# Converting three quarters of a feed-forward's weights inside the feed-forward itself, with the sums on two engines and another turn of the banks

## The chip, the cores and the metric

The kernel runs on one core of one Trainium2 chip. The metric is the device time of one execution in microseconds (us). TensorE is called PE, its weight loads PEld, VectorE is DVE, ScalarE is ACT, GpSimd is POOL, and SP is the queue that issues nearly all DMA.

## The reference

Attention with normalized queries and keys, then a feed-forward with a squared ReLU over the same tokens.

```python
batch, n_heads, seq, head_dim = (8, 12, 448, 64)
n_tokens, d_model, d_ff = (3584, 768, 2048)

q_n, k_n = rmsnorm(q, g_q), rmsnorm(k, g_k)
scores = scale * np.matmul(q_n, k_n.transpose(0, 1, 3, 2))
attn = softmax(scores)                       # written out, with 1e-9 in the denominator
x = np.matmul(attn, v)                       # (B,H,S,D) -> (B*S, H*D), in float32
h = np.maximum(x @ w_in, 0.0)
out = (h * h @ w_out).astype(np.float32)     # w_in and w_out are float64
```

The two weight matrices arrive as 64-bit floats. The kernel computes in 32-bit ones and converts the bits itself. Both matrix products of the feed-forward are done in seven block products in place of eight, which needs sums of weight blocks as well.

## The kernel before

The program has four units of two batches each. Attention of unit u runs interleaved with the feed-forward of unit u-1. Attention of unit 0 has no feed-forward beside it, and that is where all weights are converted. The four feed-forwards are called FFN 0, 1, 2 and the last one. Each has four blocks, and a block has *first products* (w_in, 14 products of 448 columns) and *second products* (w_out).

A piece is a block of 384 x 256 or 128 x 768 32-bit words (384 KB). There are 64 of them, four for each of 16 weight tiles. The conversion of a piece is a chain over four queues: a DMA loads the words, ScalarE and GpSimd split and clip them, VectorE joins them.

```python
    def split_words(n):
        ...
        low, high = words[n][:, :, :, 0], words[n][:, :, :, 1]
        nc.scalar.activation(high.bitcast(F32), high.bitcast(F32), AF.Copy, scale=REBIAS)
        nc.gpsimd.tensor_scalar(out=high.bitcast(F32), in0=high.bitcast(F32),     # the clip
                                scalar1=MOST, scalar2=-MOST, op0=ALU.min, op1=ALU.max)
        nc.scalar.activation(low.bitcast(F32), low, AF.Copy, scale=2.0**-29, bias=2.0**23)
        low_words[n] = ffn_p.tile([P, NK, P], U32, name="low", tag="part", bufs=4)
        nc.scalar.activation(low_words[n], low.bitcast(F32), AF.Copy, bias=-(2.0**23))

    def join_words(n):
        ...
            nc.vector.tensor_scalar(out=bits, in0=high, ...)                  # shift left, shift right
            nc.vector.scalar_tensor_tensor(out=bits, in0=high, ..., in1=bits) # sign
            nc.vector.tensor_tensor(out=bits, in0=bits, in1=low, op=ALU.add)
        ...
        if form == 3:                        # the fourth piece of a tile
            make_weight_forms(kind, targets.pop((kind, t)), t)   # four sums, then a store to DRAM

    def convert(n):                          # 64 times during attention of unit 0, the rest at once after it
        join_words(n - LAG)                  # LAG = 3
        load_weights(n + 2 * NT - LAG + 1)   # words: seven buffers, borrowed from acc
        split_words(n)
        make_sum()                           # one of the four sums, always on GpSimd
```

A finished tile goes to DRAM. Every feed-forward, FFN 0 too, loads its tiles from there two ahead. The products of a step turn through four PSUM banks:

```python
    def turn_roles():
        x, v_, w, y = roles
        roles[:] = w, y, v_, x               # at the start of every step
    PRODUCTS = {"P1": (0, True, ...), "P2": (2, True, ...), "P3": (1, False, ...), "P4": (3, True, ...),
                "P5": (1, True, ...), "P6": (0, False, ...), "P7": (0, False, ...)}   # role, first, ...
    FIRST_ORDER = ["P1", "P5", "P6", "P4", "P3", "P7", "P2"]
```

The feed-forward is a generator, and the main loop draws products from it between attention steps, by a cost of 2008 units for one feed-forward. This loop so also sets the order in which each engine is given its work. One place where that order shows in the trace of the kernel before: a ScalarE conversion (L574) waited 4.27 us for VectorE and ran at 94.16 us, and the exponentials issued after it ran at 94.62 us.

## Time and profile before

| | before |
|---|---|
| median of 3 runs, us | 1701.81 (1701.72 to 1702.39) |
| span of the profiled run, us | 1698.6 |
| mean granted clock of PE | 0.974 |
| attention of unit 0 with all conversions | up to 271.5 |
| FFN 0, FFN 1, FFN 2, from the last to the end, us | 386.7, 383.5, 382.1, 274.8 |

The lengths of the feed-forwards are differences between the starts of their first products in the trace. The page's totals for PE, PEld, VectorE, ScalarE and GpSimd (busy us, share of the span, instructions), and PE's waits over the whole run (what waits, for what: us in sum, times, longest), which bear on the bank turn:

```profile
PE 1567.1 (92%) x5204; PEld 710.7 (42%) x5204; DVE 794.4 (47%) x1138; ACT 552.1 (33%) x1033; POOL 643.9 (38%) x522
```

```profile
PE bank L451 <- POOL hid L423: 13.1, 7, 3.4
PE bank L402 <- DVE hid L421: 12.7, 16, 1.1
...
PE bank L451 <- DVE hid L421: 7.6, 9, 1.1
```

PE is busy 92% of the span, so there are about 130 us to win at most without fewer products or a higher clock, and most of them lie in the first 270 us. L402 is the first product, L451 the first of the second products, which needs the hidden layer (hid) complete. L402 itself does not read hid. In the program L421 reads the bank that L402 is to write next, so I take the 12.7 us to be a wait for that bank.

### The profile page before, as it was taken

What the parts mean: (1) busy time and instruction counts of PE and PEld (TensorE: products, weight loads), DVE (VectorE), ACT (ScalarE), POOL (GpSimd) and SP (SyncE); (2) the same over time, 40 slices, a digit from 0 to 9 for tenths busy, and PEclk for the clock granted to TensorE, in tenths of its full rate; (3) what the DMA queues carried; (4) which work ended last, traced back from release to release, by engine and by line L of the source; (5) the groups of instructions that cost most, each with busy time, mean ns of one, the idle gap of its engine ahead of it and who ended that gap; (6) DMA issues with size and microseconds to landing.
All of it is one profiled execution on the core that took longest, in us unless ns stands there. A gap on an engine that the chain in (4) does not pass through costs nothing.

```text
span 1698.6 us, 15053 instructions
## 1 busy us (share of the span) xinstructions
PE 1567.1 (92%) x5204; PEld 710.7 (42%) x5204; DVE 794.4 (47%) x1138; ACT 552.1 (33%) x1033; POOL 643.9 (38%) x522
## 2 busy tenths in 40 slices
PE   5877777999989999999999999999999999999997
PEld 2222222444434444444444444444444444545544
DVE  3878895334535355333535355433534344223323
ACT  5776662333231323333231323333231321220120
POOL 4666674524242245424243245434143232120211
PEclk9888888999999999999999999999999999999999
DMA  5687766222220315222221315222221314131112
GB/s 154 217 266 238 238 196 241 81 96 82 91 92 22 123 49 172 91 97 82 88 78 40 123 49 172 86 97 87 76 82 42 118 38 161 44 139 74 65 74 68
DMA packets 101081, 188.25 MB, mean 111 GB/s; under 512 B 49284, under 2 KB 83076, under 8 KB 90756
## 3 DMA queue, kind: packets, MB, share of 16 engines
q1 hardware_dynamic: 100992, 187.20, 32.6%
q8 instruction: 43, 0.70, 0.2%
q14 instruction: 42, 0.34, 0.1%
q10 hardware_dynamic: 4, 0.00, 0.0%
HBM read 152.57 MB, written 34.60 MB: 110 GB/s over the span
## 4 chain that ended last, share of the span: by engine, by line
PE 82%; DVE 6%; POOL 5%; issue 4%; DMA 2%; ACT 2%; SPq 0%; POOLq 0%; DVEq 0%; ACTq 0%
PE bank L402 28%; PE bank L468 26%; PE bank L212 9%; PE bank L272 8%; PE bank L451 5%; PE bank L191 2%; PE bank L283 2%; POOL rr L167 2%; DVE rden L294 1%; DVE hid L421 1%; PE bank L279 1%; POOL hid L423 1%; DVE out_sb L588 1%; ACT wT L214 1%; DMA in_sb<-in_forms 1%
## 5 line engine op out<-in xcount | busy, mean ns | idle before, releaser
L402 PE MATMUL bank<-xT,in_sb 128*128 128x448 f32 x1344 | 528.0, 545 | 24.8 <-DVE hid L421 12.7
L402 PEld LDWEIGHTS bank<-xT,in_sb 128*128 128x128 f32 x1344 | 249.0, 190 | 280.0 <-issue 247.9
L214 ACT ACTIVATE wT<-bank,rr 112x448 f32<-112x448 f32 x384 | 221.4, 627 | 429.7 <-PE bank L212 428.1
L423 POOL TENSOR_TENSOR hid<-hid 128x448 f32<-128x448 f32 x128 | 120.3, 950 | 472.6 <-ACT hid L422 472.6
L167 POOL TENSOR_TENSOR rr<-ms,minus_half 112x16 f32<-112x16 f32 x48 | 152.1, 3169 | 360.8 <-DVE ms L163 350.3
L468 PE MATMUL bank<-out_sb,hid 128*128 128x384 f32 x768 | 274.6, 487 | 0.0
L500 DVE TENSOR_TENSOR acc<-acc,bank 128x384 f32<-128x384 f32 x324 | 173.8, 551 | 205.7 <-PE bank L468 164.7
L212 PE MATMUL bank<-qT,kT 64*112 64x448 f32 x768 | 218.4, 621 | 52.7 <-DVE qT L193 43.0
L294 DVE RECIPROCAL rden<-bank 128x448 f32<-128x448 f32 x48 | 142.0, 2957 | 156.0 <-PE bank L283 128.9
L468 PE MATMUL bank<-out_sb,sums 128*128 128x384 f32 x576 | 212.4, 491 | 0.0
L272 PE MATMUL bank<-wT,vt 112*64 112x448 f32 x768 | 197.9, 596 | 2.2 <-DVE xT L304 2.1
L468 PEld LDWEIGHTS bank<-out_sb,hid 128*128 128x128 f32 x768 | 144.7, 190 | 103.1 <-issue 5.3
L409 ACT COPY part<-bank 128x448 f32<-128x448 f32 x128 | 68.1, 532 | 329.7 <-PE bank L402 329.7
L421 DVE TENSOR_TENSOR hid<-bank,part 128x448 f32<-128x448 f32 x128 | 76.4, 618 | 202.8 <-PE bank L402 202.0
L468 PEld LDWEIGHTS bank<-out_sb,sums 128*128 128x128 f32 x576 | 105.6, 190 | 81.9 <-issue 13.4
L422 ACT ACTIVATE hid<-hid 128x448 f32<-128x448 f32 x128 | 72.4, 577 | 198.1 <-DVE hid L421 198.1
L212 PEld LDWEIGHTS bank<-qT,kT 64*112 64x112 f32 x768 | 60.0, 182 | 171.4 <-issue 90.2
L230 DVE TENSOR_TENSOR sum<-sum,wT 112x448 f32<-112x448 f32 x72 | 65.1, 904 | 140.0 <-ACT wT L214 137.1
L451 PE MATMUL bank<-out_sb,hid 128*128 128x384 f32 x256 | 91.5, 510 | 23.1 <-POOL hid L423 13.1
L230 POOL TENSOR_TENSOR sum<-sum,wT 112x448 f32<-112x448 f32 x72 | 87.8, 1220 | 59.3 <-ACT wT L214 56.2
L272 PEld LDWEIGHTS bank<-wT,vt 112*64 112x64 f32 x768 | 39.6, 139 | 139.0 <-issue 128.6
L193 DVE TENSOR_SCALAR qT<-bank,g 128x448 f32<-128x448 f32 x48 | 32.7, 682 | 120.1 <-PE bank L191 120.1
(53 smaller groups left out, 1093.1 us busy)
## 6 DMA issues: line engine op xcount, KB each, us to landing
out_sb<-out_forms SPq DMA_DIRECT2D x32, 1536.0 KB, 9.3
in_sb<-in_forms SPq DMA_DIRECT2D x32, 1344.0 KB, 6.0
words<-in_moe_w_in_dram SPq DMA_DIRECT2D x32, 384.0 KB, 4.4
words<-in_moe_w_out_dram SPq DMA_DIRECT2D x32, 384.0 KB, 4.4
out_forms<-out_sb SPq DMA_DIRECT2D x8, 1536.0 KB, 6.5
qk<-in_q_dram SPq DMA_DIRECT2D x48, 224.0 KB, 2.8
qk<-in_k_dram SPq DMA_DIRECT2D x96, 112.0 KB, 3.0
vt<-in_v_dram SPq DMA_DIRECT2D x48, 224.0 KB, 2.7
```

Source lines behind the costliest of these rows:

```text
L167: nc.gpsimd.tensor_tensor(out=rr.rearrange("p x r -> p (x r)"), in0=ms, in1=minus_half.to_broadcast([CP, 4 * NJ]), op=ALU.pow,)
L212: nc.tensor.matmul(sc, lhsT=kT[r, ts(m, CP)], rhs=qT[r, :], start=True, stop=True)
L214: nc.scalar.activation(weights[i, e, m], sc, AF.Exp, scale=normal[i][2][:, 2 * m + e : 2 * m + e + 1])
L230: engine.tensor_tensor(out=sums[i, e], in0=sums[i, e], in1=weights[i, e, m], op=ALU.add)
L272: nc.tensor.matmul(av[ds(e * D, D), :], lhsT=values[i][:, e, m, :], rhs=weights[i, e, m], start=m == 0, stop=m == NJ - 1,)
L294: nc.vector.reciprocal(out=rden, in_=den)
L402: nc.tensor.matmul(ps, lhsT=w_sb[:, c, IN.index(left), :], rhs=forms[u, c][right], start=first and c == 0, stop=c == NK - 1, skip_group_ch ...
L421: nc.vector.tensor_tensor(out=dst, in0=ps, in1=part, op=op)
L423: nc.gpsimd.tensor_tensor(out=dst, in0=dst, in1=dst, op=ALU.mult)
L451: nc.tensor.matmul(ps, lhsT=flat[a][:, t, ds(FULL, P)], rhs=w_sb[t][:, 2 * a + half, :], start=a == 1 and t == 0, stop=a == 0 and t == 1,)
L468: nc.tensor.matmul(ps, lhsT=lefts[left][:, t, ts(tt, P)], rhs=w_sb[t][:, OUT.index(right), :], start=first and t == 0, stop=t == 1, skip_g ...
L500: nc.vector.tensor_tensor(out=acc, in0=acc, in1=ps, op=ALU.add)
```

## The change

The intent is to take conversions out of the stage in which every engine waits for another, and to do them where VectorE, ScalarE and GpSimd have room (busy for 44, 30 and 35% of FFN 0 before). Sixteen pieces (block 0's four tiles) stay in the first stage, one each 2.4 attention steps. The other 48 are drawn into FFN 0, one each 18 cost units (3.43 us on the average of FFN 0), straight into the tile that FFN 0 then uses. FFN 0 no longer loads its weights from DRAM, and finished tiles are still stored for the later ones.

```diff
     def load_in(n):
-        if n < B // 2 * NF // 2:
+        if NF // 2 <= n < B // 2 * NF // 2:         # load_out alike
...
-    def turn_roles():
+    def turn_roles(order):
         x, v_, w, y = roles
-        roles[:] = w, y, v_, x
+        roles[:] = (y, v_, w, x) if order is FIRST_ORDER else (w, y, v_, x)
...                                                  # and called at the end of a step
-        words[n] = ffn_p.tile([P, NK, P, 2], U32, name="words", tag="acc", bufs=2 * NT + 1)
+        words[n] = ffn_p.tile([P, HALF, 2], U32, name="words", tag="words")     # two buffers
...
-        low_words[n] = ffn_p.tile([P, NK, P], U32, name="low", tag="part", bufs=4)
-        nc.scalar.activation(low_words[n], low.bitcast(F32), AF.Copy, bias=-(2.0**23))
+        nc.scalar.activation(low, low.bitcast(F32), AF.Copy, bias=-(2.0**23))
...
+        (in_sb if kind == "in" else out_sb)[t] = dst       # the tile is used where it was made
...
-    def make_sum():
-        if sums_to_make:
+    def make_sums():
+        for engine in (nc.vector, nc.gpsimd) if sums_to_make else ():
             to, left, right, op = sums_to_make.popleft()
-            nc.gpsimd.tensor_tensor(out=to, in0=left, in1=right, op=op)
-            if len(sums_to_make[0]) == 2:
-                nc.sync.dma_start(*sums_to_make.popleft())
+            engine.tensor_tensor(out=to, in0=left, in1=right, op=op)
+        if sums_to_make and len(sums_to_make[0]) == 2:
+            nc.sync.dma_start(*sums_to_make.popleft())
...
+    def convert(more):
+        make_sums()
+        if begun:
+            join_words(begun.pop())
+        if more:
+            n = next(pieces)
+            load_weights(n + 1)
+            split_words(n)
+            begun.append(n)
...
+    early = deque(conversions(4, 0, 2.4))
+    block, product = COST // NBLK, 7 * COST_IN
+    late = deque(conversions(2, product + 2 * COST_IN, COST_IN))
+    for blk in range(1, NBLK):
+        late.extend(conversions(4 if blk < NBLK - 1 else 2, blk * block + 1, COST_IN))
...
                     spent += next(stream)
+                    while u == 1 and late and late[0][0] <= spent:
+                        convert(late.popleft()[1])
```

The layout of in_sb, the order of the four sums and the numbers of wT (12 to 10) and xT (33 to 32) buffers change as well. The words can't keep the buffers of acc, because FFN 0 uses those itself.

## The prediction

> **What bounds the kernel now.** I read the 40 slices of the span first, because they show where the regimes change.
>
> ```profile
> PE   5877777999989999999999999999999999999997
> DVE  3878895334535355333535355433534344223323
> ACT  5776662333231323333231323333231321220120
> PEclk9888888999999999999999999999999999999999
> ```
>
> A slice is 42.5 us. The first seven are another program than the rest: there PE is busy 70 to 80% at a clock of 0.8 to 0.9, with VectorE at 80 to 90%. From slice 8 on PE is at 90% or more and at full clock, and the other engines are half idle. So only the first 270 us, and what PE still waits for afterwards, can be shortened. Then I asked for busy time by stage: the stage of attention and weight conversion, the first feed-forward (FFN 0), and the second one.
>
> ```profile
> core 0: us, PE busy (x) PEld busy (x) DVE busy (x) ACT busy (x) POOL busy (x), PEclk, DMA share, GB/s
> 23.20:250.00 226.80, 174.26 (x652) 55.18 (x652) 183.68 (x258) 160.49 (x318) 149.81 (x147) 0.87 0.70 226
> 271.50:658.20 386.70, 376.43 (x1265) 171.79 (x1265) 169.38 (x239) 115.14 (x210) 135.99 (x101) 0.99 0.28 95
> ...
> 658.20:1041.70 383.50, 373.11 (x1264) 170.28 (x1264) 172.64 (x245) 115.13 (x210) 144.84 (x107) 1.00 0.27 91
> ```
>
> In the first stage VectorE is busy 184 of 227 us (81%), yet no engine is full: they wait on one another in turn. Who stops PE there is in the waits of PE up to 440 us:
>
> ```profile
> PE bank L212 <- DVE qT L193: 43.0, 12, 6.0
> PE bank L191 <- POOL qn L172: 13.9, 3, 9.1
> PE bank L402 <- DMA in_sb<-in_forms: 11.5, 1, 11.5
> ```
>
> Once for each pair of heads the scores wait 3.6 us for VectorE to copy qT out of its bank, because conversions stand ahead of that copy. FFN 0 then begins with a wait of 11.5 us for weights that come back from DRAM. What fills VectorE, ScalarE and GpSimd in that stage is in the groups by form, up to 265 us:
>
> ```profile
> L568 POOL TENSOR_SCALAR words<-words 128x384 f32<-128x384 f32 x64 | 37.6, 589 | 60.2 <-ACT words L567 60.2
> L574 ACT ACTIVATE low<-words 128x384 uint32<-128x384 f32 x64 | 35.8, 559 | 28.2 <-DVE in_sb L592 14.5 <-DVE out_sb L592 11.8
> L615 POOL TENSOR_TENSOR in_sb<-in_sb 128x384 f32<-128x384 f32 x32 | 35.5, 1109 | 11.4 <-DVE in_sb L592 11.4
> L588 DVE SCALAR_TENSOR_TENSOR out_sb<-words,out_sb 128x384 uint32<-128x384 uint32 x32 | 26.2, 819 | 1.1
> L592 DVE CUSTOM_DVE_ANT_0 out_sb<-out_sb,low 128x768 uint16<-128x768 uint16 x32 | 25.5, 797 | 2.0
> L584 DVE TENSOR_SCALAR out_sb<-words 128x384 uint32<-128x384 uint32 x32 | 17.0, 530 | 0.0
> ```
>
> All 64 pieces are converted there. With the rows of in_sb, a piece costs VectorE (17.2+17.0+21.9+26.2+21.1+25.5)/64 = 2.0 us, ScalarE 3 x 0.555 = 1.67 us, and GpSimd 0.59 us plus one sum of 1.1 us.
>
> [...]
> - [...] 0.87 is granted in the stage with the long waits, 1.00 in the dense one. [...]
> - [...] in the order of time L588 and L592 take 0.56 us alone and up to 1.24 us beside GpSimd[...].
> - [...] at 94.16 us a ScalarE conversion that had waited 4.27 us for VectorE ran before the exponentials of the next scores. This is the danger in the change.
> - [...] Over the whole run the first product of a feed-forward step waits 12.7 us in 16 waits for the hidden layer's evacuation.
>
> **The change, part by part.**
>
> (a) *First stage.* 16 of 64 pieces stay, one every 2.4 of 48 attention steps. VectorE's joins fall from 61 pieces to 16 in the window 23.2 to 250: 90 us less of its 184. What is left for a pair of heads (four steps): VectorE 2.96 (reciprocal) + 1.3 + 0.3 + 0.68 + 0.61 = 5.9 us, plus 1.67 pieces x 2.4 us = 9.9 us, so below PE. PE is then the bound. In the order of time around 42 to 53 us, at full clock, a plain step repeats every 2.6 us; the step with the turn of kT takes 3.8 us with its wait; the step with qT takes about 4.1 us. That is 13.1 us a pair. I add 0.7 us for joins that still stand before a qT copy (about half the pairs, 2 us each, in part hidden)[...]: 14.3 us. Before, 12 pairs take 226.8 us, 18.9 us each. Gain 12 x 4.6 = 55 us. The stretch from 250 to the first feed-forward product at 271.5 holds the 11.5 us wait for DRAM; the tiles are now used where they were made, so it goes: 11 to 12 us more. FFN 0 starts near 204 instead of 271.5: **-67 us** (50 to 85).
>
> (b) *FFN 0 takes 48 pieces.* They come one each 18 of 2008 cost units, and 383.5 us/2008 x 18 = 3.43 us. VectorE's own work in the first products of a block is about 0.35 (13.51 of 47.60 and 15.98 of 45.10 us, 18.8 of 45.6), or 1.2 us in that time. A piece adds 2.0 us and half a sum of some 0.75 us: 2.4 us. Together 3.6 us of work in 3.43 us. ScalarE has 1.0 + 1.67 = 2.7 us, GpSimd 1.2 + 0.6 + 0.55 = 2.4 us: they fit. So VectorE becomes the bound for these stretches, which are 1060 of the 2008 units. If it can run 90% full, a piece takes 4.0 us: 0.57 us x 48 = 27 us lost. **+28 us** (10 to 60).
>
> (c) *Words have two buffers.* A load may start only when the join before the last has ended, and its split on ScalarE comes one conversion later. The loop is split and clip 1.25 us, join 1.5 to 2.0 us, DMA 3.4 to 4.9 us to landing (read by windows), for two pieces: 3.1 to 4.1 us a piece. It is about as slow as VectorE, so I count it in the upper part of (b), not twice. The store of a finished tile (1344 KB, 5.8 us) stands ahead of each fourth load.
>
> (d) *Bank turn.* The first product of a step takes the bank of P4, copied long ago, instead of that of P2, evacuated last. This removes L402's 12.7 us and part of L451's 7.6 us on VectorE; L451's 13.1 us on GpSimd's square is a wait for data and stays. **-8 us**. It also gives VectorE the slack that (b) needs.
>
> (e) *Fewer weight buffers* (10 for 12): the new tile takes what the step before freed, and PE has run that before the new scores. 0 us. Loads of eight in and eight out tiles in FFN 0 go; they were hidden, apart from the first.
>
> Sum: 1701.8 - 67 + 28 - 8 = 1655.
>
> **Rivals.**
> 1. *FFN 0 gives it all back.* ScalarE stands at the head of its queue waiting for words, and the copies that free PE's banks stand behind. For: two buffers, a landing of up to 4.9 us, stores on the same queue[...]. Against: a copy of a product is needed only one or two products later, 2.2 to 4.5 us, so a ScalarE lag of 3 us is mostly absorbed. If the loop takes 4.9 us a piece, the loss is 70 us and the time about 1695.
> 2. *The conversions hide in FFN 0.* VectorE is at 44% over FFN 0 (169 of 387 us), and 48 x 2.4 = 115 us more makes 74%. With the new bank slack PE may never wait: 0 to 10 us lost, and 1630. Against: the average hides that the pieces come in stretches.
> 3. *The first stage stays slow*, bound by the chain of squares, GpSimd's power (3.1 us) and qn, or by qT behind the reciprocal (2.96 us) and a join. Then a pair takes 16 us, the gain is 47 us and the time 1675.
>
> **Range and chances.** The two large terms are unsure by some 17 and 25 us, nearly independent: about 30 us together. I take 1628 to 1690. The 2% line is at 1668, 13 us above my figure: faster 0.68, within 2% 0.29, slower 0.03.
>
> **What would show it.** (a) the first feed-forward product at 195 to 215 us, the clock before it above 0.92, L212's wait for qT under 25 us, no wait for in_sb from DRAM. (b) FFN 0 400 to 430 us long against 386.7, VectorE 65 to 75% over it, new PE waits of L402 on VectorE or ScalarE in it, and FFN 1 at 378 to 383 us. (c) ScalarE waiting for DMA of words by more than 40 us in sum would speak for rival 1. (d) L402's wait for hid under 4 us after FFN 0. The prediction is wrong if FFN 0 loses under 10 or over 60 us, or if a pair in the first stage takes over 16 us.

In (a) the 14.3 us a pair are 13.1 + 0.7 + 0.5 us; the 0.5 us, an allowance for a lower clock, was a guess. It is about 6 us over twelve pairs. The forecast itself stays: 1701.8 - 67 + 28 - 8 = 1655 us.

What the trace of the kernel before does show: PE was idle from 206.8 to 210.2 us, was granted a clock of 0.50 from there to 217.0 us, and of 1.00 from 217.0 to 223.8 us. Of its 64 instructions of L588, the 26 with no GpSimd instruction running at the same time took 0.56 us each; the other 38 took 0.88 us on average and 2.63 us at most. The 1.5 us for a join in (c) is one such undisturbed join of a w_out piece (L584, L588, L592: 0.35 + 0.56 + 0.56 us, from 93.99 us on).

## The result, and the profile after

| | before | after |
|---|---|---|
| median of 4 runs, us | 1701.76 (1699.97 to 1702.39) | 1708.47 (1706.47 to 1709.54) |
| span of the profiled run, us | 1698.6 | 1707.0 |
| first product of FFN 0 at | 271.5 | 208.6 |
| FFN 0 | 386.7 | 468.6 |
| FFN 1, FFN 2, last to end | 383.5, 382.1, 274.8 | 381.3, 377.6, 270.9 |

The ratio is 1.004, with a 95% interval of 1.0022 to 1.0057, so the times are the same within 2%. Here and below a ratio is the mean time of one kernel's fast runs over that of the other's fast runs of the same rounds, so not quite the ratio of the medians.

The sum closes: -62.9 (the earlier start) + 81.9 (FFN 0) - 2.2 - 4.5 - 3.9 = +8.4 us of span. Nothing failed in the first stage, and nothing was lost to the later feed-forwards. FFN 0 gave it all back.

The 40 slices of the changed kernel (42.7 us each, tenths of busy time, granted clock in the last line):

```profile
PE   5888897978969989999998999999998999999997
...
DVE  2654546476676556343534445343535444213323
ACT  4554443452441423333131223333132221220120
...
PEclk9999998988989989999999999999999999999999
```

VectorE's 8 and 9 tenths of the first slices are gone and the clock there is 0.9. In their place the sixth to the sixteenth slice, which are FFN 0, show PE at 6 to 9 with the clock dipping to 0.8, where before stood 9s with one 8. VectorE is at 7 at most in them.

The busy times of three stretches: the eleven pairs of heads of the first stage, FFN 0, and FFN 1.

```profile
core 0: us, PE busy (x) PEld busy (x) DVE busy (x) ACT busy (x) POOL busy (x), PEclk, DMA share, GB/s
23.10:186.80 163.70, 142.36 (x592) 46.96 (x592) 87.40 (x122) 89.74 (x166) 60.75 (x45) 0.93 0.37 109
208.60:677.20 468.60, 404.10 (x1266) 182.59 (x1264) 286.31 (x410) 182.89 (x354) 201.01 (x177) 0.92 0.33 108
677.20:1058.50 381.30, 374.99 (x1266) 171.97 (x1264) 172.70 (x245) 115.13 (x211) 144.56 (x106) 0.99 0.27 91
```

A pair of heads now takes 163.7/11 = 14.9 us, where the prediction had 14.3. FFN 0 and FFN 1 run the same 1266 matmuls, and FFN 0 takes 87 us more. Of these PE is idle for 64.5 - 6.3 = 58 us, and for 404.1 - 375.0 = 29 us it is busy longer with the same work, at a clock of 0.92 against 0.99. So each microsecond of added wait came with half a microsecond of slower work (29 to 58).

The blocks of FFN 0 one by one, from the second products of block 0 to the first products of block 3 (second and first in turn; the header is that of the lines above):

```profile
255.20:317.30 62.10, 50.43 (x169) 23.99 (x168) 36.74 (x47) 24.03 (x48) 22.84 (x18) 0.92 0.26 87
317.30:375.10 57.80, 50.09 (x139) 21.40 (x138) 36.56 (x57) 31.47 (x63) 30.20 (x30) 0.88 0.50 157
375.10:439.70 64.60, 53.07 (x169) 24.57 (x167) 42.17 (x60) 16.65 (x31) 23.33 (x20) 0.92 0.26 88
439.70:495.20 55.50, 48.78 (x143) 21.37 (x142) 38.90 (x55) 30.78 (x62) 24.14 (x26) 0.94 0.45 141
495.20:562.50 67.30, 53.32 (x165) 25.30 (x164) 43.25 (x64) 17.65 (x34) 29.92 (x23) 0.87 0.29 96
562.50:620.30 57.80, 48.30 (x142) 21.02 (x141) 30.53 (x46) 27.40 (x54) 23.62 (x24) 0.88 0.38 131
```

Against the run without late conversions (e3, below) the three stretches of first products lose 40 us and the three of second products 46 us, although only four pieces a block are split there.

In FFN 0 VectorE is at 286.3/468.6 = 61%, ScalarE at 39%, GpSimd at 43%, and DMA at 33%. No engine is full. What they wait for in FFN 0 (selected lines, in the order of the sums):

```profile
ACT words L568 <- DMA words<-in_moe_w_in_dram: 56.0, 16, 13.9
...
ACT words L568 <- DMA words<-in_moe_w_out_dram: 44.1, 13, 12.4
...
PE bank L212 <- ACT wT L214: 38.7, 10, 9.5
...
DVE sum L230 <- ACT wT L214: 32.3, 14, 7.9
...
DVE out_sb L583 <- POOL words L569: 30.3, 12, 6.1
...
PE bank L451 <- POOL hid L424: 20.3, 7, 7.8
```

ScalarE stands for 100 us at the head of its queue with a split (L568) whose words are not there. Behind it stand the exponentials (L214), and PE waits 38.7 us for those before it may write new scores. VectorE's sums (L230) wait for the same exponentials, and behind them stand the joins. PE's other new wait is for hid at the start of the second products. The two are 59 us. FFN 1 has 6.0 us of the wait for hid too, so they make 53 of the 58 us of added idle time.

The same in the order of time, in the middle of block 1's first products, which run from 317.3 to 375.1 us (start, duration, engine, line, instruction; in brackets the idle time before it and what ended it):

```profile
347.19 0.33 SPq L619 DMA_DIRECT2D out_forms<-out_sb  x1
...
347.72 0.67 DVE L591 CUSTOM_DVE_ANT_0 out_sb<-words,out_sb 128x768 uint16<-128x768 uint16 x1
...
348.42 0.33 SPq L554 DMA_DIRECT2D words<-in_moe_w_out_dram  x1
...
354.59 0.55 ACT L568 ACTIVATE words<-words 128x384 f32<-128x384 f32 x1 [6.65 <-DMA words<-in_moe_w_out_dram]
...
356.10 1.12 ACT L214 ACTIVATE wT<-bank,rr 112x448 f32<-112x448 f32 x2
356.76 1.14 PE L212 MATMUL bank<-qT,kT 64*112 64x448 f32 x3 [0.30 <-ACT wT L214]
```

The load at 348.42 could not be issued earlier: its buffer was read by a join that ended at 348.39 (347.72 + 0.67). A store of a whole tile had been issued at 347.19 on the same queue, and the words landed 6.1 us after their issue, where 3.2 us is the median in FFN 0. ScalarE waited 6.65 us, and its next exponentials ran only at 356.10.

I followed all 48 late pieces through the trace in this way. From the start of the split to the end of the clip takes 2.40 us (1.15 when nothing is in the way), from there to the join's start 1.0, the join 2.16, the next issue 0.07, and from the issue to the split of that load 4.3 on average. (A load with a store of a tile ahead of it, about one in four, landed 5.5 to 7.1 us after its issue.) The sum is 9.9 us, and two buffers go round in it, so a piece can come each 5.0 us. Measured is one each 5.26 us within a stretch (44 intervals), against the planned 3.43: (5.26 - 3.43) x 48 = 88 us, about the loss of FFN 0, which e3 below puts at 85.

That sum proves nothing alone. The terms follow one another along a buffer, so they must add up to about two intervals, and pieces are drawn as PE's work proceeds, so whatever slows a stretch lengthens its intervals. The mean also mixes two regimes: between splits that start during first products the interval is 4.78 us, for those that start during second products 6.56. The cause has to come from the runs that change one term.

What became of the first stage's wait and of the bank wait (a line of PE's waits up to 270 us, and L402's group on the page):

```profile
PE bank L212 <- DVE qT L193: 19.9, 12, 3.8
```

```profile
L402 PE MATMUL bank<-xT,in_sb 128*128 128x448 f32 x1344 | 526.8, 546 | 2.5 <-DVE xT L304 2.5
```

The wait of the scores for qT fell from 43.0 to 19.9 us. L402 no longer waits for hid at all.

### The profile page after: what moved, and what is told of

Same layout as the page of the kernel before. It is cut to its first block, busy times and chain, and to the rows that moved or that the text cites. A ratio compares the mean times of both kernels' runs of the same rounds, so it can differ in the third digit from the quotient of the medians.

```text
span 1707.0 us, 14931 instructions
## 1 busy us (share of the span) xinstructions
PE 1573.1 (92%) x5204; PEld 719.2 (42%) x5204; DVE 808.6 (47%) x1170; ACT 554.3 (32%) x1033; POOL 614.1 (36%) x490
## 4 chain that ended last, share of the span: by engine, by line
PE 72%; DVE 7%; issue 6%; POOL 6%; DMA 5%; ACT 3%; SPq 0%; POOLq 0%; ACTq 0%; DVEq 0%
PE bank L468 24%; PE bank L402 23%; PE bank L212 9%; PE bank L272 8%; PE bank L451 3%; DMA words<-in_moe_w_in_dram 3%; DMA words<-in_moe_w_out_dram 3%; PE bank L191 2%; DVE rden L294 2%; POOL rr L167 2%; POOL hid L424 2%; PE bank L279 1%; PE bank L283 1%; ACT wT L214 1%; ACT words L568 1%
## 5 line engine op out<-in xcount | busy, mean ns | idle before, releaser
L402 PE MATMUL bank<-xT,in_sb 128*128 128x448 f32 x1344 | 526.8, 546 | 2.5 <-DVE xT L304 2.5
L214 ACT ACTIVATE wT<-bank,rr 112x448 f32<-112x448 f32 x384 | 222.7, 628 | 438.8 <-PE bank L212 434.9
L402 PEld LDWEIGHTS bank<-xT,in_sb 128*128 128x128 f32 x1344 | 251.3, 192 | 255.5 <-issue 241.1
L468 PE MATMUL bank<-out_sb,hid 128*128 128x384 f32 x768 | 274.7, 487 | 2.1 <-DVE acc L501 2.1
L212 PE MATMUL bank<-qT,kT 64*112 64x448 f32 x768 | 220.3, 613 | 60.4 <-ACT wT L214 38.7
L212 PEld LDWEIGHTS bank<-qT,kT 64*112 64x112 f32 x768 | 62.8, 179 | 176.9 <-issue 77.0
L451 PE MATMUL bank<-out_sb,hid 128*128 128x384 f32 x256 | 100.7, 537 | 34.9 <-POOL hid L424 34.9
L230 DVE TENSOR_TENSOR sum<-sum,wT 112x448 f32<-112x448 f32 x72 | 65.1, 904 | 122.8 <-ACT wT L214 120.1
L230 POOL TENSOR_TENSOR sum<-sum,wT 112x448 f32<-112x448 f32 x72 | 85.1, 1182 | 55.4 <-ACT wT L214 52.3
L569 POOL TENSOR_SCALAR words<-words 128x384 f32<-128x384 f32 x64 | 40.9, 640 | 156.7 <-ACT words L568 156.7
```

Of the source, the lines that this page charges most:

```text
L212: nc.tensor.matmul(sc, lhsT=kT[r, ts(m, CP)], rhs=qT[r, :], start=True, stop=True)
L214: nc.scalar.activation(weights[i, e, m], sc, AF.Exp, scale=normal[i][2][:, 2 * m + e : 2 * m + e + 1])
L230: engine.tensor_tensor(out=sums[i, e], in0=sums[i, e], in1=weights[i, e, m], op=ALU.add)
L402: nc.tensor.matmul(ps, lhsT=w_sb[:, IN.index(left), c, :], rhs=forms[u, c][right], start=first and c == 0, stop=c == NK - 1, skip_group_ch ...
L451: nc.tensor.matmul(ps, lhsT=flat[a][:, t, ds(FULL, P)], rhs=w_sb[t][:, 2 * a + half, :], start=a == 1 and t == 0, stop=a == 0 and t == 1,)
L468: nc.tensor.matmul(ps, lhsT=lefts[left][:, t, ts(tt, P)], rhs=w_sb[t][:, OUT.index(right), :], start=first and t == 0, stop=t == 1, skip_g ...
```

## The experiments

The theory was: the loop of two word buffers sets FFN 0's pace, because it crosses the queues of three engines and a DMA, and the exponentials that stand behind ScalarE's waiting split carry the delay to PE (after the change, the split that waited 6.65 us ran at 354.59 us, the exponentials at 356.10, and PE's next scores at 356.76). The first rival was the prediction's own: VectorE is the bound. Later rivals were the store ahead of the load, and the places at which pieces are drawn. Every kernel was timed in 4 runs, beside 7 or 8 of the kernel before (medians 1700.01 to 1700.28). By the line of 2%, only e3, e6, e8 and e10 are faster than before, e5 is unclear and the rest are the same; no interval of theirs holds 1, so the smaller differences are real too. Floor means FFN 0 of e3, 383.4 us.

| run | what | us | ratio to before | FFN 0 starts | FFN 0 lasts |
|---|---|---|---|---|---|
| e1 | before, new bank turn only | 1682.62 | 0.989 | 270.1 | 382.2 |
| e3 | no late conversions (wrong result) | 1620.42 | 0.952 | 204.3 | 383.4 |
| e2 | up to five word buffers | 1678.85 | 0.987 | 205.9 | 442.2 |
| e4 | load ahead of the store | 1684.88 | 0.992 | 200.3 | 453.0 |
| e5 | a piece each 22 units | 1668.35 | 0.981 | 209.2 | 428.0 |
| e6 | no late word loads (wrong result) | 1656.71 | 0.975 | 203.8 | 421.4 |
| e7 | one of three join operations (wrong result) | 1688.31 | 0.993 | 204.3 | 453.2 |
| e9 | other places for the pieces | 1671.49 | 0.984 | 203.4 | 435.8 |
| e8 | e2, e4 and e9 together | 1639.80 | 0.964 | 202.6 | 405.0 |
| e10 | e8, places tuned | 1641.32 | 0.966 | 204.2 | 406.8 |
| e11 | clip on VectorE | 1706.96 | 1.005 | 203.7 | 470.6 |

### e1: the bank turn alone

```diff
 # the kernel before
-        roles[:] = w, y, v_, x
+        roles[:] = (y, v_, w, x) if order is FIRST_ORDER else (w, y, v_, x)
 # and turn_roles called at the end of a step instead of its start
```

> The kernel before with the other bank turn and nothing else. In the trace of the changed kernel the second, third and fourth feed-forward are 2.2, 4.5 and some 4 us shorter than before (381.3 against 383.5, 377.6 against 382.1). If that comes from the turn alone, this kernel takes 1687 to 1693 us, and its product P1 of a feed-forward step (L402) no longer waits for the hidden layer's evacuation (12.7 us before). Rival: those few us come from the lighter DMA and the other layout of the tiles; then this kernel stays at 1699 to 1703 us.

Measured: 1682.62 us, ratio 0.9893 (0.9876 to 0.9909), so -17.7 us. FFN 0, 1, 2 and the last one became 4.5, 2.6, 4.7 and 4.0 us shorter. Of PE's waits for hid, this is what is left in e1:

```profile
PE bank L450 <- POOL hid L423: 20.6, 20, 4.3
```

L402's 12.7 us are gone, and L450 (the former L451) still waits 20.6 us, as much as the 13.1 + 7.6 of before: that wait is for data, and this turn of the banks did not remove it. The time is 4 us under the expected 1687 to 1693, and the rival (1699 to 1703) is out. The waits account for 12.7 of the 17.7 us. The other 5 us are not in any single line, and I leave them open. What follows is that the rest of the change *costs* 1708.5 - 1682.6 = 26 us beside this gain.

### e3: no conversions in FFN 0 (wrong result)

```diff
-        if NF // 2 <= n < B // 2 * NF // 2:
+        if 2 <= n < B // 2 * NF // 2:       # tiles from 2 on are loaded, as copies of tiles 0 and 1
-                    while u == 1 and late and late[0][0] <= spent:
-                        convert(late.popleft()[1])
```

> Wrong result on purpose: the changed kernel without any conversion in the first feed-forward; the tiles 2 to 7 are copies of tiles 0 and 1 read back from DRAM, as many loads as the kernel before had. It gives the floor. If the loss in the first feed-forward (82 us) is all due to the late conversions and nothing else changes, that feed-forward takes 378 to 384 us and the whole 1618 to 1630 us. If part of the loss has another cause (the deferred layout, the smaller pools of weights and x tiles), it takes 400 us or more and the whole over 1640 us.

Measured: 1620.42 us, ratio 0.9524 (0.9509 to 0.954). FFN 0, on the window of its length:

```profile
204.30:587.70 383.40, 375.37 (x1267) 172.19 (x1265) 174.68 (x242) 114.74 (x210) 141.44 (x105) 0.99 0.25 84
```

The floor is 383.4 us at a clock of 0.99, with the new buffers and the new turn. That is as expected (1618 to 1630). So the 48 late pieces cost 1708.5 - 1620.4 = 88 us, 85 of them in FFN 0, and the smaller numbers of wT and xT buffers cost nothing that shows (382.2 us in e1). The rest of the change is worth 80 us, where the prediction had 75.

### e2: five word buffers

The sums of the hidden layer (tags S0 to S2) are idle during the first products. This run lends their three tiles to the words there, so that up to five pieces have a buffer; during the second products there are two as before.

```diff
-        words[n] = ffn_p.tile([P, HALF, 2], U32, name="words", tag="words")
+        words[n] = ffn_p.tile([P, HALF, 2], U32, name="words", tag=tag, bufs=2 if tag == "words" else 1)
...
+            free = [t for t in ['S0', 'S1', 'S2'] if lending[0] and n in lendable and t not in tags]
+            if not free and tags.count("words") < 2:
+                free = ["words"]
```

> The changed kernel, but while a block's first products run (35 of the 48 late pieces) the loads of words may also use the three tiles S1, S2, S4, which are idle then: five buffers in place of two, and loads run up to four pieces ahead. VectorE, ScalarE and GpSimd do the same work. Theory W (two buffers: ScalarE stands at the head of its queue waiting for words, a loop of split, join and load of 5.2 us a piece): the first feed-forward falls from 469 us to 400 to 425, ScalarE's wait for words from 100 us to under 40, the time to 1645 to 1665 us. Theory V (VectorE is the bound in these stretches): the joins still pace it, the first feed-forward stays over 445 us, the time over 1685 us.

Measured: 1678.85 us, ratio 0.9869 (0.9853 to 0.9886). That lies between the two theories, as does FFN 0 with 442.2 us; ScalarE's wait for words fell to 46.6 us and not under 40. FFN 0 is 26 us shorter than after the change. Block by block the first products went back to the floor or near it: 43.2, 47.5 and 49.2 us in blocks 1 to 3, against 43.2, 43.7 and 44.0 in e3 and 57.8, 55.5 and 57.8 after the change. The second products did not: 61.5, 70.1 and 67.8 us in blocks 0 to 2, against 47.8, 47.6 and 52.6 in e3. The stretch that ends with the first products of block 1, and the first 39 us of its second products:

```profile
303.50:356.60 53.10, 53.10 (x177) 23.27 (x174) 40.86 (x60) 33.60 (x67) 26.50 (x25) 1.00 0.51 162
356.60:396.00 39.40, 23.84 (x60) 10.10 (x59) 27.33 (x33) 13.04 (x26) 19.41 (x19) 0.78 0.28 93
```

With enough buffers PE is busy for all of 53.1 us at full clock, and VectorE reaches 77% in that stretch and ScalarE 63% without stopping it. The splits of the first products come each 3.62 us instead of 4.78. So two buffers, and not VectorE, held PE up there. VectorE was not free of the matter, though: in this stretch joins ended one each 3.42 us (ten intervals from 323.03 to 357.18 us), while PE needs 43.2/14 = 3.09 us for a product, which is 18 units. Its lag grew, and is called in later. In the second stretch every engine is less busy, PE 61% at a clock of 0.78. Two instructions of it:

```profile
363.88 2.93 PE L451 MATMUL bank<-out_sb,hid 128*128 128x384 f32 x4 [6.47 <-POOL hid L424]
```

```profile
385.48 0.54 ACT L568 ACTIVATE words<-words 128x384 f32<-128x384 f32 x1 [14.04 <-DMA words<-in_moe_w_in_dram]
```

Two things happen there. The second products need the whole hidden layer at once, so PE meets the lag that VectorE and GpSimd have gathered; and then the pieces are back at two buffers, and ScalarE waits 14 us for one load. So the number of buffers was one cause, and the place where the pieces lie is another.

### e4: the load ahead of the store

```diff
             split_words(n)
             begun.append(n)
+        store_sums()              # the store of a finished tile, taken out of make_sums
```

> The changed kernel with the store of a finished tile issued after the load of the next words in place of ahead of it. In the trace of the changed kernel a load behind a store lands 5.6 to 7 us after its issue and others after 3.2 us, for 12 tiles. If that store costs what it delays (3 us, 12 times), the time falls by 25 to 35 us, to 1675 to 1683 us. Rival: the next load then stands behind the same store, and the loop of two buffers only shifts the delay by a piece: 1700 us or more.

Measured: 1684.88 us, ratio 0.9915 (0.9894 to 0.9935). The time from a load's issue to its split fell from 4.3 to 3.97 us on average, the interval of the pieces from 5.26 to 4.89, and FFN 0 from 468.6 to 453.0. After the change, a load of 384 KB issued after a tile's store landed late (5.5 to 7.1 us instead of 3.2), and in e4 the same load issued before it landed after 3.5 to 3.8 us. The rival in the expectation was partly right: twice the next load stood behind the store instead (7.3 and 6.5 us). The time is 2 us above the expected range. One reordered line is worth 24 us, of which 16 lie in FFN 0 and 8 in its earlier start. (The starts of the other runs without this edit go from 203.4 to 209.2, so the 8 need not all be its own.)

### e5: a slower pace

```diff
-    late = deque(conversions(2, product + 2 * COST_IN, COST_IN))
+    late = deque(conversions(2, product + 2 * COST_IN, 22))
...                                # 22 for COST_IN (18) in the other blocks too
```

> The changed kernel with a late conversion each 22 cost units (4.2 us at the undisturbed rate) in place of 18 (3.43 us); nothing else. Theory W (the loop of two buffers, 5.2 us a piece as the trace of the changed kernel shows): it still paces the stretches, so the loss shrinks by 48 x 0.77 = 37 us, to some 48 us: first feed-forward 425 to 440 us, time 1665 to 1680 us, ScalarE's wait for words 50 to 70 us. If the loss were a fixed cost per piece[...] and no loop, it would not shrink with a slower pace: the time stays over 1695 us.

Measured: 1668.35 us, ratio 0.9814 (0.9794 to 0.9835). FFN 0 is 41 us shorter although the same 48 pieces are in it. The pieces come each 5.32 us now, as without this edit (5.26), and 4.81 us during first products (4.78), so the loop was not quicker. But each piece now has 22 units of other work beside it, 4.2 us of undisturbed FFN 0, so only 1.1 us of the loop stands bare instead of 1.8. PE's wait for exponentials fell from 38.7 to 4.3 us. ScalarE's wait for words is 78.2 us, more than the 50 to 70 expected. This is what a fixed loop predicts: asking faster than the loop can go makes it no faster, and leaves less work to hide it.

### e6: no loads of words in FFN 0 (wrong result)

```diff
+        if n > 16:
+            words[n] = kept[n % 2]        # the old contents, converted again
+            return
```

> Wrong result on purpose: the changed kernel, but from the 18th piece on the words are not loaded; splits and joins run on the two tiles that are there. All work of VectorE, ScalarE and GpSimd and its order stay, and so does the rule that a split waits for the join before the last; only the load's latency (3.2 to 7 us) is gone. If the latency of loads is the whole loss (85 us over the floor of 383 us that the run without late conversions showed): first feed-forward 383 to 400 us, time 1620 to 1640 us. Theory B (VectorE falls behind in the first products and the lag is paid where the second products wait for the hidden layer, as the run with five buffers suggests: 14, 22 and 15 us lost in the second products of the first three blocks): some 40 to 55 us stay: first feed-forward 425 to 440 us, time 1660 to 1675 us.

Measured: 1656.71 us, ratio 0.9751 (0.9729 to 0.9773). FFN 0 takes 421.4 us, so of the 85 us over the floor 47 need the loads and 38 do not. That is between the two expectations, closer to theory B. The interval fell to 4.06 us, not to 3.43. PE's idle time over the floor is then 27 us and its slower clock 11 us. What is left is the chain split, clip, join through three queues, and 22.5 us of waits of the second products for hid (6.0 at the floor).

### e7: one of three join operations (wrong result)

```diff
-            nc.vector.scalar_tensor_tensor(...)
-            nc.vector.tensor_tensor(out=bits, in0=bits, in1=low, op=ALU.add)
+            if n < 16:
+                nc.vector.scalar_tensor_tensor(...)
+                nc.vector.tensor_tensor(out=bits, in0=bits, in1=low, op=ALU.add)
```

> Wrong result on purpose: the changed kernel with one instead of three VectorE operations in a late join (0.45 us in place of 2.1 us); loads, buffers, splits, clips, sums and stores as they are. Theory B with W (VectorE's queue is what makes the loop long and what is late at the second products): the loop falls to (1.2 + 0.5 + some wait + 4.1)/2, about 3.2 us, below the 3.43 us pace, and the lag at the second products goes: first feed-forward 385 to 405 us, time 1622 to 1642 us. If it is the loads and stores alone that ScalarE waits for, whatever VectorE does: first feed-forward over 420 us, time over 1655 us.

Measured: 1688.31 us, ratio 0.9925 (0.9908 to 0.9941), far from the 1622 to 1642 us for theory B with W, and within the other branch (over 1655). The join fell from 2.16 to 0.58 us, which is 76 us of VectorE's time less, and FFN 0 became 15 us shorter. What the two engines wait for during FFN 0 in e7:

```profile
ACT words L568 <- DMA words<-in_moe_w_in_dram: 48.5, 13, 14.6
...
DVE out_sb L583 <- POOL words L569: 43.9, 13, 7.8
DVE in_sb L583 <- POOL words L569: 43.3, 15, 7.0
```

VectorE, now with far less to do, waits 87 us for clips, and ScalarE still waits 86.5 us for words (48.5 for those of w_in, 38.0 for those of w_out). The interval is 4.89 us. VectorE's own work is not the bound. The miss taught me that the join is one term of five in the loop, and that making it shorter moves some of the wait to another term: from issue to split takes 4.8 us now instead of 4.3.

### e9 and e8: other places, alone and with the rest

In the middle blocks twelve of sixteen pieces come one each 18 units from the block's start; the other four come in the second products, from 60 units after their start and one each 36.

```diff
+        start, before, after = ..., (4, 12, 12, 8)[blk], (4, 4, 4, 0)[blk]
+        at = [start + COST_IN * n for n in range(before + (0 if after else 3))]
+        at += [blk * block + 2 * product + 60 + 36 * n for n in range(after)]
```

> The changed kernel with the places of the late conversions alone moved: 12 of a block's 16 pieces early in its first products, 4 later in its second ones, as in the fastest kernel so far; but two buffers of words and the store ahead of the load, as changed. Theory: the loop of two buffers still costs what the five buffers saved in the first products (9 to 15 us a block there, 26 us in all) and the stores what they delayed, but the lag at the start of the second products shrinks (51 us to 20): the time 1660 to 1680 us. If the places do it all and buffers and stores nothing, it equals the fastest kernel, 1637 to 1645 us.

> A correct kernel from what the runs showed: the changed kernel with five buffers while the first products run, the store after the load, and the conversions kept away from the start of the second products: 12 of a block's 16 pieces early in the first products, 4 from 60 cost units after them, each 36 units. If the loss comes from the loop of two buffers and from VectorE's lag at that start, both shrink: first feed-forward 390 to 412 us and the time 1622 to 1648 us, under all kernels so far. If not, it stays at 1665 us or more.

Measured: e9 (places only, two buffers) 1671.49 us, ratio 0.9837 (0.9817 to 0.9857), FFN 0 33 us shorter. Its first products are still slow (58.5, 55.5 and 56.8 us): there the two buffers rule. Its second products are 47.7, 52.4 and 58.5 us, near the floor (47.8, 47.6 and 52.6). e8 has all three mends and computes the right result: 1639.80 us, ratio 0.9644 (0.9628 to 0.966), the fastest correct kernel here. Its FFN 0, and two of the waits in it:

```profile
202.60:607.60 405.00, 380.45 (x1267) 173.68 (x1265) 278.20 (x410) 182.62 (x354) 200.42 (x177) 0.98 0.38 125
```

```profile
PE bank L451 <- POOL hid L424: 16.4, 5, 7.0
...
ACT words L568 <- DMA words<-in_moe_w_in_dram: 13.5, 6, 4.1
```

VectorE does nearly the same work as after the change (278.2 against 286.3 us) in 405 us, at 69%, and ScalarE's 100 us of waiting have shrunk. The mends alone bring back 26, 16 and 33 us of FFN 0, which would be 75; together they bring 64, so they overlap. 22 us over the floor remain. The wait for hid at the start of the second products (16.4 us, 6.0 at the floor) is part of that. What was lost against the floor, in the first products of blocks 1 to 3 and the second products of blocks 0 to 2, shows the two causes apart:

| run | first products, us lost | second products, us lost |
|---|---|---|
| after | 40 | 46 |
| e2, buffers alone | 9 | 51 |
| e9, places alone | 40 | 11 |
| e8, both and the later store | 6 | 16 |

More buffers mend the first products alone, and other places the second products alone.

### e10: the places tuned

```diff
-        ..., (4, 12, 12, 8)[blk], (4, 4, 4, 0)[blk]
+        ..., (4, 11, 11, 8)[blk], (4, 5, 5, 0)[blk]
-        at += [blk * block + 2 * product + 60 + 36 * n for n in range(after)]
+        at += [blk * block + 2 * product + 56 + 34 * n for n in range(after)]
```

> The fastest kernel so far (five buffers, store after load, conversions away from the boundary) with one more piece of blocks 1 and 2 moved to the second products: 11 and 5. Its feed-forward is 405 us against the floor of 383, most of it in the second products of blocks 1 and 2 (56.7 and 59.3 us against 47.6 and 52.6). If VectorE's lag at their start is what is left, one piece less ahead of it saves 2 to 6 us: 1634 to 1639 us. If the pieces in the second products cost it, it gets 2 to 5 us slower.

Measured: 1641.32 us, ratio 0.9656 (0.9633 to 0.9679): no gain over e8, a miss. Moving one more piece across the boundary does not reach the remaining 22 us. How much of the lag at the boundary is VectorE's and how much GpSimd's stays open.

### e11: the clip on VectorE

```diff
-        nc.gpsimd.tensor_scalar(
+        (nc.gpsimd if n < 16 else nc.vector).tensor_scalar(
```

> The changed kernel with the clip of the late pieces on VectorE in place of GpSimd; nothing else. In the trace of the changed kernel the clip ends 2.4 us after the split has begun, where 1.15 us would do without other work on GpSimd (its power takes 3.1 us), and VectorE waits 54.5 us for clips. Theory F[...]: the loop gets about 1 us shorter for two pieces, the time falls by 10 to 30 us to 1680 to 1698 us, although VectorE has 48 x 0.5 us more to do. If VectorE's own load is what counts, the time rises by 5 to 25 us, to 1712 us or more.

Measured: 1706.96 us, ratio 1.0047 (1.0026 to 1.0067), FFN 0 470.6 us: as after the change, and outside both expectations (1680 to 1698, or 1712 and more). Theory F put the 2.40 us down to other work that GpSimd does ahead of the clip. From the split's start to the clip's end fell from 2.40 to 1.95 us, but from there to the join grew from 1.0 to 1.44 and the join from 2.16 to 2.39. The interval went from 5.26 to 5.35. GpSimd's queue was not the cause by itself: the delay moved to the other queue.

### All runs against one sum

If the loop sets the pace in the stretches with pieces, FFN 0 is 48 intervals plus what lies outside of them. A unit is 383.4/2008 = 0.191 us at the floor. At 18 units a piece, 2008 - 48 x 18 = 1144 units or 218 us lie outside; at 22 units, 952 or 182 us.

| run | interval, us | 48 intervals + outside | measured |
|---|---|---|---|
| after | 5.26 | 252 + 218 = 470 | 468.6 |
| e4 | 4.89 | 235 + 218 = 453 | 453.0 |
| e7 | 4.89 | 235 + 218 = 453 | 453.2 |
| e11 | 5.35 | 257 + 218 = 475 | 470.6 |
| e2 | 4.54 | 218 + 218 = 436 | 442.2 |
| e6 | 4.06 | 195 + 218 = 413 | 421.4 |
| e5 | 5.32 | 255 + 182 = 437 | 428.0 |

The intervals are measured in each run, and any loss in a stretch lengthens them, so this is a check of where the time lies, not a forecast and no proof of the loop. To within 9 us the loss lies in the stretches with pieces, in every one of these runs. What speaks for the loop is the interval during first products alone: 4.78 us after the change, and nearly the same with a slower pace (e5, 4.81), other places (e9, 4.80) and the clip elsewhere (e11, 4.78); a little less with the load first (e4, 4.40) and a short join (e7, 4.45); and far less with five buffers (e2, 3.62) or no loads (e6, 3.51). e8 to e10 have pieces at other distances and are left out.

## Why the prediction was wrong

The time came out at 1708.5 us, above the range of 1628 to 1690, though within 2% of before.

**(a) The first stage** was right. FFN 0 starts 63 us earlier (predicted 67), at 208.6 us; the clock before it is 0.93, the wait for qT 19.9 us (predicted under 25), and the 11.5 us wait for in_sb from DRAM is gone. A pair takes 14.9 us (predicted 14.3), so rival 3 (16 us) did not come. Of the 4.0 us that a pair gained, 2.4 are idle time of PE and 1.6 are busy time, of which the clock (0.93 for 0.87) explains 0.9 by my estimate, if busy time goes with the inverse of the clock, as it does from FFN 1 to FFN 0 after the change (374.99 x 0.99/0.92 = 403.5 us; measured 404.10). So a removed wait paid at most 1.65 times here.

**(d) The bank turn** was right in mechanism and too small: e1 shows 17.7 us where 8 were predicted. L402's wait for hid fell to zero as said. **(e) The buffers** cost nothing, as e3's floor shows.

**(b) and (c) are the step that failed.** The failed sentence is in (c): the loop of the words takes "3.1 to 4.1 us a piece", is "about as slow as VectorE", and so I counted it "in the upper part of (b), not twice". The loss by the 48 pieces was put at 28 us. e3 measures it as 88. The loop is 5.26 us on average and 4.78 during first products. Its engine terms were taken at their undisturbed length: split and clip 1.25 us, where they take 2.40 with the wait for GpSimd's queue; no time from the clip to the join, where it is 1.0; the join 1.5 to 2.0, where it is 2.16. The landing of 3.4 to 4.9 us does hold the 4.3 from issue to split, but at its upper end, with the store ahead of a quarter of the loads; the store was named, and given no time. The planned 3.43 us was an average of FFN 0 as well: most pieces lie in first products, where 18 units took 45.1/14 = 3.2 us by the prediction's own lines. And VectorE at 3.6 us of work in 3.43 us was not what stopped PE: e2 runs the first products of block 1 at PE's full speed at the same pace, and e7 takes 76 us of work off VectorE for 15 us of FFN 0. The new waits of L402 that (b) expected did not come: in FFN 0 PE waits for exponentials (L212, 38.7 us) and for hid at the second products (L451, 20.3 us).

The loop may also lengthen itself. A late load blocks ScalarE's queue, so the exponentials come late. VectorE's sums then wait for those exponentials, so the joins behind them come late, and the next load with them. Each link is a line in the waits of FFN 0 (100.1 us of ScalarE, 32.3 of VectorE, 38.7 of PE). That they feed back is argued from the order in which the program issues this work. No run shows it alone: e5, which relieves ScalarE's queue, kept the interval of 5.3 us, and that speaks against a large share.

**Rival 1** had the mechanism: a loop of 4.9 us, 70 us lost, 1695 us. Measured are 5.26 (4.78 during first products), 88 and 1708. My argument against it was that a lag of 3 us of ScalarE is mostly absorbed; the lags were up to 13.9 us. The criterion for it, over 40 us of ScalarE's waits for words, came out at 100.1. **Rival 2** counted mean loads, and those were right (286.3 us of VectorE, which is 74% of the old 386.7 us and 61% of the longer FFN 0), yet said nothing of the time. Two small readings were off as well and changed nothing: slice 12 of the kernel before shows PE at 8, not 9, and the longest L588 beside GpSimd took 2.63 us, not 1.24. One part was in nobody's account: the second products as a meeting point, where the lag of two engines is called in (46 us after the change, 11 in e9).

## What to carry to other kernels

Before moving work beside a busy engine, write down the loop of each small buffer, with the waits for every queue that it crosses, and divide by the number of buffers; mean occupancy does not show it (no engine but PE was above 61% of FFN 0 after the change). If the loop is slower than the plan, ask for less, give it more buffers from tiles that are idle just then (here sums, 26 us), and keep large stores behind the loads that others wait for (16 us). Draw side work in stretches in which a lag may build up and shrink again, away from the point where the main work needs everything at once (33 us).
